# Storing dK and dV of heads 1 to 30 in one 2 MB DMA each, and requesting the third V after the first dV

## The chip, the cores and the metric

The kernel runs on one core of a Trainium2 chip. The core has a matrix engine (TensorE, PE in the profile; its weight loads are PEld), a vector engine (VectorE, DVE), a scalar engine (ScalarE, ACT), GpSimd (POOL) and a sync engine (SP). Sixteen DMA engines move data between the chip's main memory (HBM) and the on-chip memory. Here every DMA of the program is issued by SP. The metric is the device time of one execution in microseconds (us), the median over several runs.

## The reference

It is the forward and backward pass of attention for one query row per head (a decode step): 32 heads, 8192 keys and values per head, head size 128, everything in bf16.

```python
def _fwd_reference(q, k, v):                  # q (1,32,1,128), k and v (1,32,8192,128)
    scale = q.shape[-1] ** -0.5
    scores = jnp.einsum('bhqd,bhkd->bhqk', q, k) * scale
    attn = _softmax(scores, axis=-1)
    return jnp.einsum('bhqk,bhkd->bhqd', attn, v)

_out, _vjp = jax.vjp(_f, q, k, v)
_grads = _vjp(grad_out)                       # dq, dk, dv
```

For one head, with the scores' softmax p (8192 numbers), the outputs are o = p V, dP = V dO, ds = p (dP - dO.o) scale, dq = ds K, dK = ds q (an outer product, 8192 x 128) and dV = p dO (an outer product too). K and V are read once, 2 MB each per head; dK and dV are written once, 2 MB each per head. That makes 268 MB of traffic in all, half read, half written.

## The kernel before

**Tiling.** The 8192 rows of a head lie on 128 partitions, 64 rows to a partition, so a partition's share of K, V, dK or dV is one contiguous run of 16 KB. `Kt` has three buffers, `Vt` two, and the two generated tiles `G_dk` and `G_dv` two each. A head is cut into four quarters for the on-chip work: `outer(h, which, r)` makes quarter r of dK or dV with one VectorE instruction (L207), and `k_blocks(h, u)` transposes a quarter of K on VectorE (L142). V is transposed on TensorE (`v_transposes`, L180) and evacuated by ScalarE (L182).

**Stores.** Inside `outer`, `parts` says in how many pieces the tile is stored: 4 for the last head, otherwise `NST = 2`. So quarters 0 and 1 make the first 1 MB store and quarters 2 and 3 the second (issued at L215). Loads are whole 2 MB DMAs (L75 for K, L81 for V), other than those of head 0, which go in four pieces.

**The loop.** One iteration h works on the scores, the softmax and dV of head h, and on dK and dq of head h-1. The instructions stand in the order in which the program emits them on each engine (`tc.manual_schedule()`). VectorE's order in iteration h: the four transposes of K(h); ds of head h-1; dK quarters 0 to 3 of head h-1, with the small softmax steps of head h between them; then dV quarters 0 to 3 of head h. TensorE's: scores of head h; dq of head h-1 in two halves; softmax sums; the V transposes of head h and the product with V; dP.

**SP's order.** SP issues the DMAs in program order and, at each, waits for what that DMA needs: the data (for a store), a free buffer (for a load), and a free completion semaphore. The trace shows eight such semaphores in rotation, so a DMA can be issued when the one eight places before it has landed. In a middle iteration h the order is: first half of dK(h-1), K(h+2), second half of dK(h-1), first half of dV(h), V(h+2), second half of dV(h). `load_k(h+2)` takes the buffer of K(h-1), last read by `dq_of(h-1, 1)`; `load_v(h+2)` takes that of V(h), last read by TensorE's transposes and product of head h. In iteration 0 there is no dK; K(2) is requested late in it, and V(2) between the second and third quarter of dV(0).

**The ends.** Before the loop SP requests q, grad_out, K(0), V(0), K(1), V(1). After the last load, V(31) in iteration 29, only stores are left. Head 31 stores its dV and dK in four pieces each, and the two small outputs go through `result` (L247).

Of the kernel before, what the change touches and what calls it, by code (L numbers as in the profile page):

```python
# [16 lines left out]
R = 4  # L17
K_BUFS = 3
V_BUFS = 2
NST = 2  # L20
QD = 32


# [1 line left out]
def kernel(  # L25
# [13 lines left out]
    _, H, S, D = k.shape  # L39
# [23 lines left out]
    def rows_of(x, h, c, parts):  # L63
        L = NT // parts
        return x[0, h].rearrange("(p n) d -> p n d", p=P)[:, c * L:(c + 1) * L, :]

    def slots(X, c, parts):
        L = NT // parts
        return X[:, c * L:(c + 1) * L, :]

    def load_k(h):
        Kt[h] = kpool.tile([P, NT, D], BF16, tag="K", name="Kt")
        parts = NCH if h == 0 else 1
        for c in range(parts):
            nc.sync.dma_start(slots(Kt[h], c, parts), rows_of(k, h, c, parts))  # L75

    def load_v(h):
        Vt[h] = vpool.tile([P, NT, D], BF16, tag="V", name="Vt")
        parts = NCH if h == 0 else 1
        for c in range(parts):  # L80
            nc.sync.dma_start(slots(Vt[h], c, parts), rows_of(v, h, c, parts))  # L81
# [55 lines left out]
    def k_blocks(h, u):  # L137


        if u == 0:  # L140
            XK[h] = ktpool.tile([P, CH, NB, NCH, QD], F32, tag="XK", name="XK_sb")
        nc.vector.transpose(XK[h][:, :, :, u, :],  # L142
                            slots(Kt[h], u, NCH).rearrange("p g d -> p (g d)").bitcast(F32).rearrange(
                                "p (g w j) -> p g w j", g=CH, w=NB))

    def k_scores(h):
        x = st[h]
        x["s"] = psS.tile([P, 512], F32, tag="s", name="s_ps")
        out = x["s"][:, 0:NT].rearrange("p (a g) -> p g a", a=NQ)
        cols = XK.pop(h).rearrange("p g w u i -> p (g w u i)").bitcast(BF16).rearrange(  # L150
            "p (g w ui e) -> p g w e ui", g=CH, w=NB, e=2)
        for g in range(CH):
            for c in range(2 * NB):
                nc.tensor.matmul(out[:, g, :], lhsT=cols[:, g, c // 2, c % 2], rhs=q_blk[:, h, c, :],  # L154
                                 start=(c == 0), stop=(c == 2 * NB - 1), skip_group_check=True)

    def s_mask(h):
        x = st[h]
        x["sm"] = small.tile([P, NQ, NCH, CH], F32, tag="sm", name="sm")
        nc.vector.tensor_tensor(  # L160
            x["sm"][:], x["s"][:, 0:NT].rearrange("p (a g) -> p a g", a=NQ).unsqueeze(2)
            .to_broadcast([P, NQ, NCH, CH]),
            in_quad[:].unsqueeze(1).unsqueeze(3).to_broadcast([P, NQ, NCH, CH]), op=ALU.mult)

    def s_swap(h):

        x = st[h]
        x["sn"] = x["s"][:, 128:128 + NT]
        for a in range(NQ):
            nc.tensor.matmul(x["s"][a * QD:(a + 1) * QD, 128:128 + NT], lhsT=lane[:],  # L170
                             rhs=x["sm"][:, a].rearrange("p u g -> p (u g)"),
                             start=True, stop=True, skip_group_check=True)
# [22 lines left out]
    def contract(Xt, rep, out_col, first=0, last=NT):  # L195
        for n in range(first, last):
            nc.tensor.matmul(out_col, lhsT=Xt[:, n, :], rhs=rep[:, n, 0:1],  # L197
                             start=(n == 0), stop=(n == NT - 1), skip_group_check=True)

    def outer(h, which, r):  # L200
        x = st[h]
        if r == 0:
            x[which] = gpool.tile([P, NT, D], BF16, tag=which, name="G_" + which)
        G, dst = x[which], out_2 if which == "dk" else out_3
        rep, row = x["ds"] if which == "dk" else x["p"], x["qd"][:, 0 if which == "dk" else 1, :]
        Q = NT // 4
        nc.vector.tensor_tensor(  # L207
            slots(G, r, 4).rearrange("p n (a b) -> p n a b", b=R),
            slots(rep, r, 4).unsqueeze(2).to_broadcast([P, Q, D // R, R]),
            row.rearrange("p (a b) -> p a b", b=R).unsqueeze(1).to_broadcast([P, Q, D // R, R]),  # L210
            op=ALU.mult)
        parts = 4 if h == H - 1 else NST
        if r % (4 // parts) == 4 // parts - 1:
            c = r // (4 // parts)
            nc.sync.dma_start(rows_of(dst, h, c, parts), slots(G, c, parts))  # L215
# [9 lines left out]
    def ds_of(h):  # L225
        x = st[h]
        pdt = small.tile([P, 1], F32, tag="pdt")
        nc.vector.tensor_copy(pdt[:], x["m"][:, 1:2])  # L228
        x["ds"] = small.tile([P, NT, R], BF16, tag="dsrep", name="ds_rep")
        nc.vector.scalar_tensor_tensor(  # L230
            out=x["ds"][:], in0=x["dp"][:, 0:NT].unsqueeze(2).to_broadcast([P, NT, R]), scalar=pdt[:],
            in1=x["p_s"][:].unsqueeze(2).to_broadcast([P, NT, R]), op0=ALU.subtract, op1=ALU.mult)

    def dq_of(h, half):
        out = st[h]["dp"][:, 128:129]
        contract(Kt[h], st[h]["ds"], out, half * NT // 2, (half + 1) * NT // 2)
        if half == 1:
            nc.scalar.copy(dq_all[:, h:h + 1], out)  # L238
# [10 lines left out]
    for h in range(H + 1):  # L249
        p_ = h - 1  # L250
        if h < H:
            x = st[h] = {}
            for u in range(NCH):
                k_blocks(h, u)
            k_scores(h)
        if h > 0:
            ds_of(p_)
            outer(p_, "dk", 0)
            dq_of(p_, 0)
        if h < H:  # L260
            s_mask(h)
            s_swap(h)
        if h > 0:
            dq_of(p_, 1)
            outer(p_, "dk", 1)
        if 0 < h and h + 2 < H:
            load_k(h + 2)
        if h < H:
            mx = small.tile([P, 1], F32, tag="mx")
            nc.vector.reduce_max(mx[:], x["sn"], axis=AX.X)  # L270
            diag = small.tile([P, P], F32, tag="diag")
            nc.vector.tensor_scalar(diag[:], ident_f[:], mx[:], scale, op0=ALU.mult, op1=ALU.mult)
            x["m"] = psM.tile([P, 512], F32, tag="m", name="m_ps")
            nc.tensor.matmul(x["m"][:, 128:256], lhsT=ones_f[:], rhs=diag[:], start=True, stop=True,  # L274
                             skip_group_check=True)
            rows_bc(h)
        if h > 0:
            outer(p_, "dk", 2)
        if h == 0:
            load_k(2)  # L280
        if h < H:
            nbias = small.tile([P, 1], F32, tag="nbias")
            nc.vector.tensor_reduce(nbias[:], x["m"][:, 128:256], axis=AX.X, op=ALU.max, negate=True)  # L283
            e = small.tile([P, NT], F32, tag="e")
            rs = small.tile([P, 1], F32, tag="rs")
            nc.scalar.activation(e[:], x["sn"], ACT.Exp, bias=nbias[:], scale=scale, accum_out=rs[:])  # L286
            nc.tensor.matmul(x["m"][:, 0:1], lhsT=ones_f[:], rhs=rs[:], start=True, stop=True,  # L287
                             skip_group_check=True)
        if h > 0:
            outer(p_, "dk", 3)  # L290
        if h == H:
            break
        rinv = small.tile([P, 1], F32, tag="rinv")
        nc.vector.reciprocal(rinv[:], x["m"][:, 0:1])  # L294
        x["p"] = small.tile([P, NT, R], BF16, tag="prep", name="p_rep")
        nc.scalar.activation(x["p"][:], e[:].unsqueeze(2).to_broadcast([P, NT, R]), ACT.Copy, scale=rinv[:])  # L296
        x["p_s"] = small.tile([P, NT], F32, tag="p_s", name="p_s")
        nc.vector.tensor_scalar(x["p_s"][:], e[:], rinv[:], scale, op0=ALU.mult, op1=ALU.mult)
        v_transposes(h, 0)
        v_transposes(h, 1)  # L300
        contract(Vt[h], x["p"], x["m"][:, 2:3])
        nc.scalar.copy(o_all[:, h:h + 1], x["m"][:, 2:3])
        v_scores(h, 0)
        v_transposes(h, 2)
        nc.tensor.matmul(x["m"][:, 1:2], lhsT=do_f[:, h:h + 1].to_broadcast([P, P]), rhs=o_all[:, h:h + 1],
                         start=True, stop=True, skip_group_check=True)
        v_scores(h, 1)
        v_transposes(h, 3)
        v_scores(h, 2)
        v_scores(h, 3)  # L310
        outer(h, "dv", 0)
        outer(h, "dv", 1)
        if h + 2 < H:
            load_v(h + 2)
        outer(h, "dv", 2)
        outer(h, "dv", 3)
        if h == H - 1:
            result(o_all, out_0)

# [32 lines left out]
```

## Time and profile before

| | |
|---|---|
| median of 6 runs | 650.8 us (650.63 to 651.25) |
| the profiled execution's own time | 650.65 us |
| its span in the profile | 648.9 us |
| mean granted TensorE clock | 0.619 |
| busy share: TensorE / VectorE / ScalarE | 76% / 79% / 28% |
| DMA queue of SP: bytes, share of 16 engines' span | 268.48 MB, 98.3% |
| mean DMA rate over the span | 416 GB/s |
| loads of 2 MB | 31 of K and 31 of V, 27.2 us from issue to landing |
| stores of 1 MB | 62 of dK and 62 of dV, 25.0 and 25.2 us from issue to landing |

Times in the profile are counted from the start of the span. A busy share is an average over the whole span and says nothing of which engine waits for which; the waits and the chain of work do. A DMA is split over the 16 DMA engines, each of which posts one of sixteen increments of the DMA's semaphore; the DMA has landed when the last of them has. The records of these increments are called the semaphore events below. SPq rows are DMA issues: their time is the instant of the request, not that of the transfer.

### The profile page before, as it was taken

What the parts mean: (1) busy time and instruction counts of PE and PEld (TensorE: products, weight loads), DVE (VectorE), ACT (ScalarE), POOL (GpSimd) and SP (SyncE); (2) the same over time, 40 slices, a digit from 0 to 9 for tenths busy, and PEclk for the clock granted to TensorE, in tenths of its full rate; (3) what the DMA queues carried; (4) which work ended last, traced back from release to release, by engine and by line L of the source; (5) the groups of instructions that cost most, each with busy time, mean ns of one, the idle gap of its engine ahead of it and who ended that gap; (6) DMA issues with size and microseconds to landing.
All of it is one profiled execution on the core that took longest, in us unless ns stands there. A gap on an engine that the chain in (4) does not pass through costs nothing.

```text
span 648.9 us, 21097 instructions
## 1 busy us (share of the span) xinstructions
PE 496.2 (76%) x9705; PEld 463.9 (71%) x9705; DVE 513.6 (79%) x660; ACT 183.1 (28%) x325; POOL 0.7 (0%) x6
## 2 busy tenths in 40 slices
PE   2888888787878768797778787777877878767781
PEld 1888788676868668787668777766867877656781
DVE  5799899798777978778877788777797877887753
ACT  0333232232232222332222322223322233222330
POOL 0000000000000000000000000000000000000000
PEclk9986666577666565656565755676655566656755
DMA  8999999999999999999999999999999999999985
GB/s 336 408 388 429 422 425 425 425 425 427 424 430 425 425 427 425 428 426 429 424 425 427 425 426 427 426 428 427 424 425 427 426 432 422 425 428 425 424 363 226
DMA packets 29368, 269.82 MB, mean 416 GB/s; under 512 B 3424, under 2 KB 3424, under 8 KB 5472
## 3 DMA queue, kind: packets, MB, share of 16 engines
q1 hardware_dynamic: 29280, 268.48, 98.3%
q8 instruction: 76, 1.25, 0.7%
q14 instruction: 12, 0.10, 0.0%
HBM read 134.23 MB, written 134.23 MB: 414 GB/s over the span
## 4 chain that ended last, share of the span: by engine, by line
DMA 68%; PE 16%; DVE 10%; ACT 2%; issue 1%; SPq 0%; DVEq 0%; ACTq 0%
DMA Kt<-in_k_dram 39%; DMA out_dram<-G_dv 29%; DVE XK_sb L142 8%; PE T_ps L180 6%; PE s_ps L154 2%; PE dp_ps L197 2%; PE m_ps L197 2%; PE dp_ps L192 1%; ACT XT_sb L182 1%; PE m_ps L274 1%; DVE G_dv L207 1%; DVE G_dk L207 1%; PE m_ps L287 1%; PE s_ps L170 1%; ACT qd L223 0%
## 5 line engine op out<-in xcount | busy, mean ns | idle before, releaser
L180 PE MATMUL T_ps<-ident_f,Vt 128*128 128x128 f32 x1024 | 211.9, 385 | 0.0
L142 DVE STREAM_TRANSPOSE XK_sb<-Kt 128x1024 f32<-128x1024 f32 x128 | 148.1, 1213 | 65.0 <-DMA Kt<-in_k_dram 64.9
L180 PEld LDWEIGHTS T_ps<-ident_f,Vt 128*128 128x128 f32 x1024 | 188.3, 210 | 0.0
L182 ACT COPY XT_sb<-T_ps 128x1024 f32<-128x1024 f32 x128 | 129.6, 1013 | 136.8 <-PE T_ps L180 136.8
L207 DVE TENSOR_TENSOR G_dv<-p_rep,qd 128x2048 bf16<-128x2048 bf16 x128 | 148.2, 1219 | 14.3 <-DMA out_dram<-G_dv 10.2
L207 DVE TENSOR_TENSOR G_dk<-ds_rep,qd 128x2048 bf16<-128x2048 bf16 x128 | 155.7, 1218 | 1.1
L154 PE MATMUL s_ps<-q_blk,XK_sb 128*128 128x4 bf16 x2048 | 59.6, 168 | 61.1 <-DVE pdt L228 58.4
L154 PEld LDWEIGHTS <-XK_sb 128*128 128x128 bf16 x2048 | 57.0, 104 | 63.4 <-DVE pdt L228 60.6
L192 PEld LDWEIGHTS <-XT_sb 128*128 128x128 bf16 x2048 | 70.7, 103 | 28.5 <-ACT XT_sb L182 27.2
L192 PE MATMUL dp_ps<-do_blk,XT_sb 128*128 128x2 bf16 x2048 | 72.2, 165 | 24.5 <-ACT XT_sb L182 24.5
L197 PE MATMUL dp_ps<-ds_rep,Kt 128*128 128x1 bf16 x2048 | 64.3, 165 | 2.6 <-issue 2.1
L197 PEld LDWEIGHTS <-Kt 128*128 128x128 bf16 x2048 | 59.7, 104 | 8.1 <-issue 8.0
L238 ACT COPY dq_all<-dp_ps 128x1 f32<-128x1 f32 x32 | 5.1, 159 | 207.6 <-PE dp_ps L197 207.6
L197 PEld LDWEIGHTS <-Vt 128*128 128x128 bf16 x2048 | 60.1, 101 | 1.5
L197 PE MATMUL m_ps<-p_rep,Vt 128*128 128x1 bf16 x2048 | 58.6, 165 | 0.0
L287 PEld LDWEIGHTS m_ps<-rs,ones_f 128*128 128x128 f32 x64 | 16.0, 310 | 48.6 <-ACT e L286 48.6
L287 PE MATMUL m_ps<-rs,ones_f 128*128 128x1 f32 x64 | 18.7, 362 | 39.2 <-ACT e L286 39.2
L274 PE MATMUL m_ps<-diag,ones_f 128*128 128x128 f32 x64 | 25.6, 500 | 1.9 <-issue 1.2
L283 DVE TENSOR_REDUCE nbias<-m_ps 128x1 f32<-128x128 f32 x32 | 9.3, 291 | 20.2 <-ACT qd L223 20.2
L296 ACT ACTIVATE p_rep<-e,rinv 128x256 bf16<-128x256 f32 x32 | 16.3, 508 | 30.3 <-DVE rinv L294 30.3
L223 ACT CAST qd<-m_ps 128x256 bf16<-128x256 f32 x32 | 11.9, 372 | 44.9 <-PE m_ps L219 44.9
L230 DVE SCALAR_TENSOR_TENSOR ds_rep<-dp_ps,pdt,p_s 128x256 bf16<-128x256 f32 x32 | 15.5, 484 | 9.0 <-PE dp_ps L192 6.3
(44 smaller groups left out, 153.8 us busy)
## 6 DMA issues: line engine op xcount, KB each, us to landing
Kt<-in_k_dram SPq DMA_DIRECT2D x31, 2048.0 KB, 27.2
Vt<-in_v_dram SPq DMA_DIRECT2D x31, 2048.0 KB, 27.2
out_dram<-G_dv SPq DMA_DIRECT2D x62, 1024.0 KB, 25.2
out_dram<-G_dk SPq DMA_DIRECT2D x62, 1024.0 KB, 25.0
Kt<-in_k_dram SPq DMA_DIRECT2D x4, 512.0 KB, 5.1
Vt<-in_v_dram SPq DMA_DIRECT2D x4, 512.0 KB, 8.2
out_dram<-G_dv SPq DMA_DIRECT2D x4, 512.0 KB, 15.9
out_dram<-G_dk SPq DMA_DIRECT2D x4, 512.0 KB, 9.2
```

The lines of the kernel that those rows point to most:

```text
L142: nc.vector.transpose(XK[h][:, :, :, u, :], slots(Kt[h], u, NCH).rearrange("p g d -> p (g d)").bitcast(F32).rearrange("p (g w j) -> p g w ...
L154: nc.tensor.matmul(out[:, g, :], lhsT=cols[:, g, c // 2, c % 2], rhs=q_blk[:, h, c, :], start=(c == 0), stop=(c == 2 * NB - 1), skip_group ...
L180: nc.tensor.transpose(T_ps[:, i, :], words[:, m * P:(m + 1) * P], ident_f[:])
L182: nc.scalar.copy(X[:], T_ps[:])
L192: nc.tensor.matmul(st[h]["dp"][:, n:n + 2], lhsT=X[:, i, e2, :], rhs=do_blk[:, h, e2, :], start=(e2 == 0), stop=(e2 == 1), skip_group_chec ...
L197: nc.tensor.matmul(out_col, lhsT=Xt[:, n, :], rhs=rep[:, n, 0:1], start=(n == 0), stop=(n == NT - 1), skip_group_check=True)
L207: nc.vector.tensor_tensor(slots(G, r, 4).rearrange("p n (a b) -> p n a b", b=R), slots(rep, r, 4).unsqueeze(2).to_broadcast([P, Q, D // R, ...
L223: nc.scalar.copy(x["qd"][:].rearrange("p a d -> p (a d)"), x["m"][:, 256:512])
L230: nc.vector.scalar_tensor_tensor(out=x["ds"][:], in0=x["dp"][:, 0:NT].unsqueeze(2).to_broadcast([P, NT, R]), scalar=pdt[:], in1=x["p_s"][: ...
L274: nc.tensor.matmul(x["m"][:, 128:256], lhsT=ones_f[:], rhs=diag[:], start=True, stop=True, skip_group_check=True)
L287: nc.tensor.matmul(x["m"][:, 0:1], lhsT=ones_f[:], rhs=rs[:], start=True, stop=True, skip_group_check=True)
L296: nc.scalar.activation(x["p"][:], e[:].unsqueeze(2).to_broadcast([P, NT, R]), ACT.Copy, scale=rinv[:])
```

## The change

The constant `NST` goes. `parts` becomes 4 for head 31, 2 for head 0 and 1 for all others, so `outer` issues a single 2 MB store after quarter 3 for heads 1 to 30. In iteration h (1 to 29) `load_v(h + 2)` stands after quarter 2 of dV(h) rather than after quarter 1; in iteration 0 it stands after quarter 3, behind both halves of dV(0).

```diff
-NST = 2
...
-        parts = 4 if h == H - 1 else NST
+        parts = 4 if h == H - 1 else 2 if h == 0 else 1
         if r % (4 // parts) == 4 // parts - 1:
             c = r // (4 // parts)
             nc.sync.dma_start(rows_of(dst, h, c, parts), slots(G, c, parts))
...
         outer(h, "dv", 0)
         outer(h, "dv", 1)
-        if h + 2 < H:
+        outer(h, "dv", 2)
+        if 0 < h and h + 2 < H:
             load_v(h + 2)
-        outer(h, "dv", 2)
         outer(h, "dv", 3)
+        if h == 0:
+            load_v(2)
```

SP's order in a middle iteration h becomes K(h+2), dK(h-1), V(h+2), dV(h): four DMAs of 2 MB each in place of six. Sixty of the 206 DMAs disappear. The bytes moved, the arithmetic and the buffers stay as they are.

## The prediction

> **What bounds the kernel now.** I read the page's strip of DMA and its queue table first, then SP's issues in order of time, then the waits, then the stretches at the end.
>
> ```profile
> DMA  8999999999999999999999999999999999999985
> GB/s 336 408 388 429 422 425 425 425 425 427 424 430 425 425 427 425 428 426 429 424 425 427 425 426 427 426 428 427 424 425 427 426 432 422 425 428 425 424 363 226
> ...
> q1 hardware_dynamic: 29280, 268.48, 98.3%
> q8 instruction: 76, 1.25, 0.7%
> ```
>
> From the fourth slice to the thirty-eighth the DMA rate stands at 422 to 432 GB/s without a dip, while TensorE and VectorE are at 76% and 79%. The transfers are the bound. In SP's order of issue, one head in the middle:
>
> ```profile
> 230.27 0.33 SPq L215 DMA_DIRECT2D out_dram<-G_dv  x1
> 232.88 0.34 SPq L81 DMA_DIRECT2D Vt<-in_v_dram  x1
> 235.33 0.33 SPq L215 DMA_DIRECT2D out_dram<-G_dv  x1
> 240.19 0.33 SPq L215 DMA_DIRECT2D out_dram<-G_dk  x1
> 242.70 0.34 SPq L75 DMA_DIRECT2D Kt<-in_k_dram  x1
> 245.22 0.33 SPq L215 DMA_DIRECT2D out_dram<-G_dk  x1
> 250.09 0.33 SPq L215 DMA_DIRECT2D out_dram<-G_dv  x1
> ```
>
> Each issue falls some 0.05 us after the landing of the DMA eight places before (the one at 230.27 after K, landed at 230.21 by the semaphore events). So the gaps are the times that the earlier DMAs took in the queue: 4.86 and 4.87 us for a load of 2 MB, but 2.61 + 2.45 and 2.51 + 2.52 us for two stores of 1 MB. A head takes 19.82 us. What VectorE waits for, by the page's costliest groups (the last figures are the idle time before them), and below it the last three of the stretches by time (TensorE, weight loads, VectorE, ScalarE, POOL busy, clock, DMA share, GB/s):
>
> ```profile
> L142 DVE STREAM_TRANSPOSE XK_sb<-Kt 128x1024 f32<-128x1024 f32 x128 | 148.1, 1213 | 65.0 <-DMA Kt<-in_k_dram 64.9
> ...
> L207 DVE TENSOR_TENSOR G_dv<-p_rep,qd 128x2048 bf16<-128x2048 bf16 x128 | 148.2, 1219 | 14.3 <-DMA out_dram<-G_dv 10.2
> ```
> ```profile
> 628.00:640.00 12.00, 6.18 (x126) 5.67 (x124) 5.27 (x6) 3.03 (x7) 0.00 (x0) 0.50 0.78 315
> 640.00:644.00 4.00, 0.00 (x0) 0.00 (x0) 0.00 (x0) 0.00 (x0) 0.00 (x0) 0.50 0.67 269
> 644.00:648.80 4.80, 0.00 (x0) 0.00 (x0) 0.00 (x0) 0.00 (x0) 0.00 (x0) 0.50 0.09 38
> ```
>
> VectorE waits for K, about 2.6 us a head: compute follows the transfers. In the last stretch only 0.09 of the 16 DMA engines is at work: they do not finish together. The semaphore events say how far apart. For the last store of dV(30) the first engine is done at 616.60, the last but one at 631.52, the last at 632.41; for the very last DMA it is 641.73, 646.56 and 647.91. The last engine's landings in the tail follow at 1.23 to 1.26 us per 512 KB, so it has work up to the end. **The bound is the chain of transfers on the slowest DMA engine.** Its landing times jump at some fetches of instructions (76 of 16 KB), and it is slower at stores: over 85 DMAs from 300 to 588 us, its median per head is 4.865 and 4.867 for the loads and 2.523, 2.614, 2.480 and 2.522 for the halves (5.07 a pair). The engine that lands first takes 4.855 and 4.862, and 2.446, 2.459, 2.447 and 2.460 (4.906 a pair).
>
> **The change, part by part.** The sum is made against the profiled execution, 650.65 us (span 648.9), which is 0.15 below the median.
>
> *Sixty pairs of 1 MB stores become sixty stores of 2 MB.* The trace has no 2 MB store. Bounds from the nearest rows, for an ordinary engine: if it takes what a 2 MB load takes, 4.858, the pair's 4.906 falls by 0.048: 60 x 0.048 = 2.9 us. Extrapolated from stores alone (512 KB in 1.245 in the tail on the last engine, 1 MB in 2.453, so 1.208 per further 512 KB) it takes 4.87: 60 x 0.037 = 2.2 us. By the packets' own times (309 ns for 8 KB, 611 for 16 KB, 9 for a semaphore write; eight packets and one semaphore write per DMA and engine) 8 x 7 + 9 = 65 ns a pair: 3.9 us. On the slowest engine, 5.07 to 4.866 gives up to 0.204 a pair, 12.2 us. But that engine would soon no longer be the slowest: the next one ends 1.35 us before it (646.56 against 647.91), and that one gains only the ordinary amount. So the ceiling is the ordinary gain plus 1.35. For this the slowest engine must lose 1.35 of its extra 60 x (5.07 - 4.906) = 9.8 us, 14% of it. I take 2.9, the load's row being the nearest in size, plus 1.3: 4.2 us. Ends kept: 2.2 (nothing of the extra goes) and 5.3 (3.9 + 1.35). A loss isn't excluded; it is a rival below.
>
> Here the page "DMA: Bandwidth & Descriptors" of the Trainium skill (Anatomy of one DMA) would give far more: it fits a DMA as about 2.0 us fixed plus its bytes, which for sixty DMAs fewer is 120 us, were they to run one by one. The trace shows them back to back, with 0.05 us per extra DMA. Against the change speaks the same page's ceiling of 435 GB/s (Specifications): the stretch from 120 to 600 us runs at 426, which as an estimate leaves 480 x (1 - 426/435) = 10 us at most.
>
> *The wait of VectorE for dV.* The first quarter of dV(h) needs the buffer of dV(h-2). Before, its second half landed 12.5 us after K(h) (621.82 against 609.35 in the last iteration). In the new queue, K(h) is followed by dK(h-3), V(h), dV(h-2): about 14.7 us. VectorE reaches that quarter 12.2 us after K (621.54 against 609.38), so it now waits some 2.4 us; the four quarters take 4.63, to 19.4, and K(h+1) lands at 19.5. The wait thus replaces that of 2.6 us for K. Behind it stand the transposes of head h+1, then dK. dK's first quarter is reached 5.3 us after K, and its buffer is free at 4.9: no wait. Cost zero, covered by the depth of the queue.
>
> *The moved requests, queue by queue.* Only SP issues DMAs; POOL's queue is passed by none. V(h+2) waits for TensorE's last transposes of head h, which end 19.5 to 21.5 us after K(h) (609.01 against 589.50 and 251.70 against 230.21), and dV(h) stands behind it on SP, ready at 19.4. Then five 2 MB DMAs, 22 to 24 us of work, lie ahead of them, so the queue is not dry. Were that cover gone, each iteration would lose the lateness plus the latency of a request (about 2 us, first K: request 1.65, first landing 4.84 with 1.28 of transfer). The smallest cover is early: V(3) is issued at 46.49 behind dK(0), whose last half ends at 49.6 on the first engine and 52.8 on the last, 1.1 and 4.3 us after the transfer could start. The first half of dV(1) leaves this gap but isn't needed to fill it. SP's sixty issues of 0.33 us are hidden: SP is waiting anyway.
>
> *Iteration 0.* The second half of dV(0) goes ahead of V(2), at about 25.2 (VectorE ends that tile at 25.1) rather than 29.94. Before, V(2) was requested at 29.57, while the last engine was busy until 33.97; on the middle engine V(2) took 5.91 instead of 4.86. Gain between 0 and 1.05; I take 0, since the last engine never lacked work. V(2) lands 2.5 us later, near 43, and TensorE wants it at about 55.
>
> *The tail.* Of the queue, 16 MB now lie behind K(31) and not 15, so K(31) lands about 2.5 us earlier within the same work. The last engine was busy to the end, so this gains nothing. dK(31) is issued 25.1 us after K(31) (634.40), while the queue lasts 39: no new gap. Cost zero.
>
> Sum: 650.65 - 4.2 = 646.45, on the median's scale 646.6.
>
> **The rivals.** *The stores' extra time belongs to writing, not to the number of DMAs.* Then a 2 MB store takes what two halves take; only 60 semaphore writes of 9 ns go, 0.5 us: 650.3, no change. For it: the slowest engine's extra is in stores alone. Against: ordinary engines take 309 ns for 8 KB against 611 for 16.
>
> *16 KB packets are slower in stores.* This is the rival on the other side. K(2) took 5.19 us on the first engine where others take 4.855, V(2) 5.99; the store running between them was undisturbed at 2.53. If big stores had K(2)'s excess throughout, 5.19 instead of 5.07 (slowest) or 4.906: 60 x 0.12 to 0.28 = 7 to 17 us, 658 to 668. It decides once a 2 MB store takes over 5.07. Against it: all loads after 50 us take 4.86.
>
> *The queue runs dry behind V(h+2).* It would show as gaps after each dV. From the cover of 22 us, this needs TensorE later by more than that; only the early 1.1 us could go, below the noise.
>
> **How the numbers follow.** A kernel like this can be told from no change at about 0.2%, 1.3 us. Forecast, 0.74: 646.6, its own range 645.2 to 648.6 (gains of 5.3 to 2.2, and with up to 0.3 of the early 1.05). Writing itself, 0.13: 649.6 to 651. Slower packets, 0.11; dry queue, 0.02: both above. Faster 0.74, same 0.13, slower 0.13. The range, 644.9 to 650.9, leaves out the slower cases and a little at the bottom, which a larger part of the early 1.05 would reach.
>
> **What would show it.** In the profile after: 2 MB loads still at 4.86 us and stores of 2 MB at 4.85 to 4.95 between issues or landings; VectorE's wait for K down from 65 us to under 20, and that of G_dv for its store up from 10 to some 60; the mean rate up from 416 to 419 GB/s; the next slowest DMA engine close behind the last at the end. I am wrong if stores of 2 MB take 5.07 or more, if GB/s dips in the middle slices, or if another engine's fetches put it behind.

## The result and the profile after

The changed kernel takes 649.17 us (median of 18 runs, 648.42 to 650.02) against 650.83 us for the kernel before (38 runs, 650.33 to 652.34). The ratio is 0.9972, with a 95% interval of 0.9966 to 0.9979: faster by 1.4 to 2.2 us, where 4.2 were forecast. The profiled execution of the changed kernel took 648.37 us (span 646.6), that of the kernel before 650.65.

Nearly all that was said of the structure came. The page's strip of the DMA rate and its queue table, for the changed kernel:

```profile
GB/s 332 412 426 428 425 425 423 427 429 423 425 428 429 430 427 427 427 429 428 428 427 428 429 430 425 430 426 431 426 423 431 428 429 427 425 432 424 423 356 218
...
q1 hardware_dynamic: 20640, 268.48, 98.0%
q8 instruction: 76, 1.25, 0.7%
```

The queue moves the same bytes in 20640 packets rather than 29280, and no middle slice dips: the queue never runs dry. The page's costliest groups, where the last figures are the idle time before the instruction and what ended it:

```profile
L206 DVE TENSOR_TENSOR G_dv<-p_rep,qd 128x2048 bf16<-128x2048 bf16 x128 | 148.2, 1219 | 67.7 <-DMA out_dram<-G_dv 65.2
...
L141 DVE STREAM_TRANSPOSE XK_sb<-Kt 128x1024 f32<-128x1024 f32 x128 | 148.1, 1213 | 5.6 <-DMA Kt<-in_k_dram 5.3
```

VectorE's wait for K fell from 64.9 to 5.3 us, and its wait for the store of dV rose from 10.2 to 65.2: one wait took the place of the other, and the DMA rate did not suffer: from 120 to 600 us it is 427 GB/s (426 before). SP's issues of about one head, in time order:

```profile
308.42 0.34 SPq L80 DMA_DIRECT2D Vt<-in_v_dram  x1
308.86 0.41 SPq L214 DMA_DIRECT2D out_dram<-G_dv  x1
315.57 0.34 SPq L74 DMA_DIRECT2D Kt<-in_k_dram  x1
318.49 0.33 SPq L214 DMA_DIRECT2D out_dram<-G_dk  x1
328.01 0.34 SPq L80 DMA_DIRECT2D Vt<-in_v_dram  x1
```

Before, the issues stood 2.4 to 4.9 us apart, because each waited for the landing of the DMA eight places earlier. Now V and dV go out 0.44 us apart. The waits of SP's queue (what it waited for, total us, times, longest) say what releases them:

```profile
SPq L80 <- PE T_ps L179: 249.8, 30, 9.4
SPq L74 <- PE dp_ps L196: 176.3, 29, 8.4
SPq L214 <- DVE rinv L293: 100.3, 31, 11.6
```

SP now waits for TensorE's last read of a buffer and for VectorE's data, no longer for a DMA's completion. So the gaps between issues no longer give the duration of a DMA, and the durations below are taken from the semaphore events alone. The end, by windows (TensorE, weight loads, VectorE, ScalarE, POOL busy, clock, DMA share, GB/s), after one long window in the middle:

```profile
120.00:600.00 480.00, 384.44 (x7418) 360.05 (x7415) 388.43 (x492) 138.17 (x246) 0.00 (x0) 0.57 1.01 427
628.00:640.00 12.00, 2.37 (x67) 2.01 (x66) 5.11 (x5) 0.89 (x4) 0.00 (x0) 0.50 0.76 309
640.00:644.00 4.00, 0.00 (x0) 0.00 (x0) 0.00 (x0) 0.00 (x0) 0.00 (x0) 0.50 0.23 92
644.00:646.60 2.60, 0.00 (x0) 0.00 (x0) 0.00 (x0) 0.00 (x0) 0.00 (x0) 0.50 0.02 10
```

Here the forecast parted from the chip. The end was to fill up, with the next slowest engine close behind the last. Instead the DMA engines work at a share of 0.23 in the last 6.6 to 2.6 us and of 0.02 after that. The kernel before, counted back from its own end in the same way, has 0.29 and 0.03: the end has hardly changed, and one engine is alone in it. (A share of 0.06 is one engine of sixteen.) The semaphore events of the last DMA, and the time that a DMA engine needs from the landing of K(8) to that of K(28), twenty heads in the middle:

| | first engine done | last but one | last | first engine, 20 heads | last engine, 20 heads | difference |
|---|---|---|---|---|---|---|
| before | 641.73 | 646.56 | 647.91 | 390.74 | 399.23 | 8.49 |
| after | 639.44 | 643.15 | 645.60 | 389.16 | 399.11 | 9.95 |

In the profiled pair the ordinary engine gained 1.58 us in twenty heads and the last one 0.12. The gap between the last and the next at the end is 1.35 us before and 2.45 after. That gap differs from execution to execution: with 1 MB stores the runs below have 2.27, 1.68 and 2.82, with 2 MB stores 0.58 and 1.73, so no trend is shown in it. The twenty heads are steadier, and there the sign stays: the last engine gains less than the first. The profiled execution of the changed kernel is the fastest of its nineteen, so its end alone says little.

### The profile page after: what moved, and what is told of

It is laid out like the page before. It is cut to its first block, busy times and chain, and to the rows that moved or that the text cites. A ratio compares the mean times of both kernels' runs of the same rounds, so it can differ in the third digit from the quotient of the medians.

```text
span 646.6 us, 20978 instructions
## 1 busy us (share of the span) xinstructions
PE 500.5 (77%) x9705; PEld 468.2 (72%) x9705; DVE 513.0 (79%) x660; ACT 183.1 (28%) x325; POOL 0.7 (0%) x6
## 3 DMA queue, kind: packets, MB, share of 16 engines
q1 hardware_dynamic: 20640, 268.48, 98.0%
q8 instruction: 76, 1.25, 0.7%
## 4 chain that ended last, share of the span: by engine, by line
DMA 53%; PE 27%; DVE 14%; ACT 2%; issue 1%; SPq 0%; DVEq 0%; ACTq 0%
DMA Kt<-in_k_dram 48%; DVE XK_sb L141 10%; PE T_ps L179 8%; PE s_ps L153 6%; PE dp_ps L196 5%; DMA out_dram<-G_dv 5%; DVE G_dv L206 2%; PE m_ps L196 2%; PE dp_ps L191 2%; PE s_ps L169 1%; PE m_ps L273 1%; ACT XT_sb L181 1%; PE m_ps L286 1%; DVE G_dk L206 1%; ACT qd L222 1%
## 5 line engine op out<-in xcount | busy, mean ns | idle before, releaser
L179 PE MATMUL T_ps<-ident_f,Vt 128*128 128x128 f32 x1024 | 216.2, 391 | 0.0
L206 DVE TENSOR_TENSOR G_dv<-p_rep,qd 128x2048 bf16<-128x2048 bf16 x128 | 148.2, 1219 | 67.7 <-DMA out_dram<-G_dv 65.2
L179 PEld LDWEIGHTS T_ps<-ident_f,Vt 128*128 128x128 f32 x1024 | 191.8, 213 | 0.0
```

The source lines that it names most:

```text
L179: nc.tensor.transpose(T_ps[:, i, :], words[:, m * P:(m + 1) * P], ident_f[:])
L206: nc.vector.tensor_tensor(slots(G, r, 4).rearrange("p n (a b) -> p n a b", b=R), slots(rep, r, 4).unsqueeze(2).to_broadcast([P, Q, D // R, ...
```

## The experiments

Two questions were to be told apart: which part of the change gives the gain, merging or the order in iteration 0; and what the extra time of the slowest DMA engine depends on: the number of stores (the forecast's step), their bytes, or something else in the kernel. In the expectations, letters stand for the theories of that stage. Ratios are against the kernel before, on the same chip.

### Which part of the change

**Merging alone**: the changed kernel with iteration 0 as before.

```diff
         outer(h, "dv", 1)
+        if h == 0:
+            load_v(2)
         outer(h, "dv", 2)
...
-        if h == 0:
-            load_v(2)
```

> The merged 2 MB stores alone; in iteration 0 the order is that of before (V(2) requested between the second and third quarter of dV(0)). Theory A (the slowest DMA engine pays its extra time for the bytes that it stores, so merging leaves its 5.03 to 5.07 us per 2 MB stored nearly as they are; the gain of the change comes from iteration 0): 650.0 to 651, within 0.8 us of before, and the last landing of dK(0)'s second half at 52 to 53 us as before (50.7 in the changed kernel). Theory B (merging gives the gain): 648.5 to 649.5, like the changed kernel.

Measured: 649.1 us, ratio 0.9971 (0.9960 to 0.9981). That is the changed kernel's ratio: merging gives the whole gain.

**Iteration 0 alone**: the kernel before with the new order of iteration 0.

```diff
-        if h + 2 < H:
+        if 0 < h and h + 2 < H:
             load_v(h + 2)
         outer(h, "dv", 2)
         outer(h, "dv", 3)
+        if h == 0:
+            load_v(2)
```

> Halves as before for all heads; only iteration 0 has the changed order (both halves of dV(0), then V(2)). Theory A: 648.6 to 649.6, about as fast as the changed kernel, with V(2) taking about 4.9 us on the last DMA engine instead of 6.5. Theory B: 650.5 to 651, as before.

Measured: 650.73 us, 0.9998 (0.9989 to 1.0007). Nothing, as forecast. In the profiled execution of before, V(2) took 6.00 us on the first engine, and that engine was 0.95 us later at the last store of dV(30) than here (616.60 against 615.65). Two runs with probes, one of the kernel before and one of this one, tell whether the slow V(2) belongs to the old order. The probes, in both:

```diff
+    probe = consts.tile([16, 16, 2, D], BF16)
...
+        if h <= 14:
+            for n in (4, 5):
+                nc.sync.dma_start(probe[0:n, h, n - 4, :], q.rearrange("b h s d -> (b h s) d")[0:n, :])
```

> The kernel before, with tiny loads of 4 and 5 rows after dV of heads 0 to 14, so that the difference shows when the fifth engine's data have landed. It is the comparison for the next run: the fifth engine is expected not to be the last engine before about 100 us.

> The kernel with only iteration 0 changed, and the same tiny loads. At 45 us all engines are 1.0 to 2.4 us earlier than in the kernel before. If the fifth engine's lead is there too and is lost later, its lag to the first engine grows faster than in the run before this by 1 to 2 us within 150 us; if it never had a lead, the two runs agree on it from the start.

Measured: 650.26 and 651.13 us, one run each. V(2) took 4.61 us on the first engine in the old order, 4.5 to 4.7 in the new one. With merging alone, which has the old order too, it took 5.33. So V(2) is slow in two of three executions of the old order and in none of the new one, but the time does not follow it: the order of iteration 0 is not shown to matter. The fifth engine, which will turn out to be the last, landed at 39.44 against 39.88 us, 101.02 against 101.71, 242.35 against 243.27 and 322.67 against 323.75 in the old and the new order: no lead for the new one. In both runs it is not yet the last at 39 and 60 us, and it is from 122 us on.

With these runs the twenty heads have four executions of 1 MB stores and three of 2 MB stores:

| stores | kernels | first engine | last engine | difference |
|---|---|---|---|---|
| 1 MB | before, iteration 0 alone, both with probes | 390.72 to 390.74 | 399.23, 399.40, 399.28, 399.26 | 8.5 to 8.7 |
| 2 MB | after, merging alone, after with the probes below | 389.16, 388.99, 389.07 | 399.11, 397.77, 398.07 | 10.0, 8.8, 9.0 |

The ordinary engine gains 1.66 us in 40 pairs, 0.042 a pair, and does so evenly. The last one gains 0.2 to 1.5 on the mean of the four (399.29), 1.0 in the mean of the three. Its extra has not shrunk; it is larger by 0.1 to 1.5 us.

### The size of the stores, the other way

**Stores in quarters**: four stores of 512 KB for every head but the first.

```diff
-        parts = 4 if h == H - 1 else 2 if h == 0 else 1
+        parts = 2 if h == 0 else 4
```

> The changed kernel, with dK and dV of heads 1 to 30 stored in four 512 KB DMAs each instead of one. By the packets' own times (4 x 8 x 159 ns for 4 KB against 8 x 611 ns) a 2 MB store costs an ordinary engine 0.2 us more. Theory A in its form 'extra per byte on top of the packets': the slowest engine goes from 5.05 to about 5.25 per 2 MB and the kernel is 12 us slower than the changed one, about 661. Theory A in its form 'a rate limit of that engine's stores, whatever the packets': the slowest engine stays near 5.05 to 5.1, other engines come up to it, and the time is 649 to 653. Theory C (an extra per DMA): the extra grows fourfold, over 20 us slower.

Measured: 676.05 us, 1.0395 (1.0378 to 1.0412), far above both. The middle window of this kernel and two of its SP waits:

```profile
120.00:600.00 480.00, 360.53 (x6950) 336.66 (x6946) 365.79 (x458) 130.07 (x230) 0.00 (x0) 0.57 1.01 404
```
```profile
SPq L214 <- DMA Vt<-in_v_dram: 137.0, 29, 6.3
SPq L214 <- DMA Kt<-in_k_dram: 132.8, 29, 7.0
```

The rate is 404 GB/s at a full DMA share. With eight semaphores in rotation, SP waits for the loads among the last eight DMAs, and eight DMAs now hold some 6.4 MB (ten make the 8 MB of a head; before, six did). The quarters took 1.24 to 1.25 us on the first engine and on the last (1.25 to 1.30 just behind a load), and the 2 MB loads 5.3 to 5.5 in the mean instead of 4.86, on both: here it is the loads that are slow, and no run shows why. So the run does not answer the question: the mix changed with the size. It only shows that the 180 DMAs more than in the changed kernel cost 0.15 us each, not 0.04.

### Which engine is the last

**Tiny loads** of 1 to 15 rows after dV in heads 14 to 28 of the changed kernel; the one of n rows has n data increments.

```diff
+    probe = consts.tile([16, 16, D], BF16)
...
+        if 14 <= h <= 28:
+            n = h - 13
+            nc.sync.dma_start(probe[0:n, n, :], q.rearrange("b h s d -> (b h s) d")[0:n, :])
```

> The changed kernel with one tiny load per head more in heads 14 to 28, of 1, 2, ... 15 rows, to see which DMA engine lands last: a DMA of n rows is expected to run on n engines, so it posts n semaphore events, and the one event that is new from n to n+1 shows the lag of the engine added. If the slowest engine is the sixteenth, none of the 15 has its lag of 8 to 15 us; otherwise the lag appears at the n that adds it. The time should stay within 1 us of the changed kernel.

Measured: 648.54 us, one run. A load of n rows shows n late increments and one update at the issue. That agrees with the Trainium skill, "DMA: Bandwidth & Descriptors" (Why a DMA increments its semaphore by 16 and not by 1): a DMA issued from SP uses the largest number of engines, up to 16, that divides its outer dimension, and of the sixteen the lowest-numbered ones. The trace shows how many engines take part, not which; the numbers of the engines here rest on that page. By it each row count adds one engine to those of the last. Engines 1, 2, 3, 8 and 9 are nearly level, the fourth lags some 3 to 5 us behind the first, the fifth 11 and rising to 15, the sixth, seventh and tenth to sixteenth 10 to 14. **Ten engines lag as a group, six do not, and the fifth is the last.**

**Taking work from the fifth engine**: dV(15) stored as partitions 0 to 67 and 68 to 127, which by the same rule run on 4 and on 15 engines.

```diff
+            if (h, which) == (15, "dv"):
+                for lo, hi in ((0, 68), (68, P)):
+                    nc.sync.dma_start(rows_of(dst, h, c, parts)[lo:hi], slots(G, c, parts)[lo:hi])
+            else:
+                nc.sync.dma_start(rows_of(dst, h, c, parts), slots(G, c, parts))
```

> The changed kernel, with dV of head 15 stored in two DMAs, of partitions 0 to 67 and 68 to 127. If a DMA runs on the largest number of engines up to 16 that divides its count of partitions, 68 go to four engines (17 partitions each) and 60 to fifteen (4 each): engines 1 to 4 get 21 packets of 16 KB instead of 8 (7.9 us more), the others 4 or none (2.4 to 4.9 us less). Theory A (the end is set by the fifth engine, which is last, and the four first ones have 11 to 15 us to spare): 649.2 - 2.4 = 646.8. Theory D (the end is set by all engines together, or by the compute): 649 to 650, no gain.

Measured: 653.31 us, 1.0039 (1.0025 to 1.0052): slower. The events confirm 4 and 15 engines. But the four landed that store 10.9 to 19 us after the one before it, where 17 packets of 0.611 us would take 10.4, and two of them lagged 19.9 and 21.5 us afterwards: they became the last.

**The control**: the same split at partition 64, on all 16 engines, `((0, 64), (64, P))`.

> The same split store, but of partitions 0 to 63 and 64 to 127: both run on 16 engines, 4 packets each, and no engine gets more or less. Theory A: as the changed kernel, 649.2 within 0.8. If it is faster by 2 us, the gain of the uneven split is not from unloading the last engine.

Measured: 651.64 us, 1.0014 (1.0005 to 1.0023), 2.5 us above the changed kernel's 649.17 for one store in two pieces. On the last engine in the profiled execution the pieces took 2.57 and 2.66 us and the DMA after them 6.24 instead of about 4.9. **Two such stores**, dV(15) and dK(20) split 68 and 60, `in ((15, "dv"), (20, "dk"))`:

> The uneven split twice, dV of head 15 and dK of head 20. Theory A: engines 1 to 4 get 15.9 us more; the fourth, which was some 11 us ahead of the last, becomes the last by about 5: 649.2 + 5 = 654, slower than with none and than with one. Theory D: no such turn, 647 or less or unchanged.

Measured: 676.4 us, 1.0387 (1.0364 to 1.0410). At K(24) the last engine lags 38.4 us behind the first, against 12.4 in the changed kernel: that is nearly all of the 27 us. A store cut by partitions has a price of its own, whose cause no run here shows, so these three runs could not test the unloading of one engine. They gave no faster version either.

### What the extra depends on

The next kernels keep the transfers and take the computation away: K and V are loaded in the changed kernel's order, whole stores write zeros, and two VectorE copies of one column per head wait for the loads. dQ, dK, dV and the output are not computed.

**Transfers alone, whole stores.**

```diff
+    def store(which, h):
+        dst = out_2 if which == "dk" else out_3
+        dst = dst[0, h].rearrange("(p n) d -> p n d", p=P)
+        L = NT // PIECES
+        for c in range(PIECES):
+            nc.sync.dma_start(dst[:, c * L:(c + 1) * L, :], G[which][:, c * L:(c + 1) * L, :])
...
+        nc.vector.tensor_copy(seen[:, 0, h:h + 1], t["K", h][:, NT - 1, D - 1:D])
+        nc.vector.tensor_copy(seen[:, 1, h:h + 1], t["V", h][:, NT - 1, D - 1:D])
+        if 0 < h and h + 2 < H:
+            load(k, kpool, "K", h + 2)
+        if h > 0:
+            store("dk", h - 1)
+        if h + 2 < H:
+            load(v, vpool, "V", h + 2)
+        store("dv", h)
```

> The transfers of the changed kernel without its arithmetic: K and V of all heads loaded and 2 MB of zeros stored for each dK and dV, in the order K, dK, V, dV, so the outputs are not computed. Few instructions, so hardly any fetches. If the extra of the fifth engine's stores (5.00 to 5.09 us against 4.87) belongs to that engine, one engine lags by some 64 x 0.17 = 11 us at the end and the time is about 640; if it needs the compute or the fetches, all engines end together within 2 us at 628 to 632.

Measured: 632.43 us, 0.9719 (0.9701 to 0.9737). Its queues, its SP issues and two windows (VectorE, POOL busy, clock, DMA share, GB/s):

```profile
q1 hardware_dynamic: 18528, 268.46, 99.8%
q14 instruction: 2, 0.02, 0.0%
```
```profile
303.65 0.34 SPq L70 DMA_DIRECT2D out_dram<-G_dk  x1
308.64 0.33 SPq L63 DMA_DIRECT2D Vt<-in_v_dram  x1
313.37 0.34 SPq L70 DMA_DIRECT2D out_dram<-G_dv  x1
318.25 0.33 SPq L63 DMA_DIRECT2D Kt<-in_k_dram  x1
323.11 0.34 SPq L70 DMA_DIRECT2D out_dram<-G_dk  x1
```
```profile
120.00:560.00 440.00, 7.03 (x45) 0.00 (x0) 1.00 1.01 431
625.00:630.60 5.60, 0.00 (x0) 0.00 (x0) 1.00 0.28 114
```

There is no q8 row: nothing fetches TensorE's instructions. All DMAs stand 4.7 to 5.0 us apart, the rate is 431 GB/s, and the engines end within 3.1 us of each other. So with no computation there is no laggard, and the transfers alone are 17 us shorter than the kernel.

**Transfers alone, halves**: `PIECES = 2`.

> The transfers alone as in the run before this (zeros stored, nothing computed), but every dK and dV in two 1 MB stores. By the first-landing engine's rows (4.906 against 4.858 per 2 MB) it is 64 x 0.048 = 3.1 us slower than with whole stores (632.4), about 635.5; by the packets' times (65 ns a pair) 4.2 us, 636.6. If halves cost nothing when no compute runs, 632 to 633.

Measured: 635.33 us, 0.975 (0.9725 to 0.9774): 2.9 us more for 64 more DMAs, 0.045 a pair. This is the price of the forecast's first term (0.048), measured by itself.

**Transfers and TensorE**: some 300 products per head on constants, the first on K(h), as many instructions as the kernel's.

```diff
+        nc.tensor.matmul(acc[:, 0:4], lhsT=t["K", h][:, 0, :], rhs=ident[:, 0:4], start=True, stop=True,
+                         skip_group_check=True)
+        for i in range(302):
+            nc.tensor.matmul(acc[:, 4:8], lhsT=ident[:], rhs=ident[:, 0:4], start=True, stop=True,
+                             skip_group_check=True)
```

> The transfers alone, whole stores, plus some 300 matrix products per head on constants, as many TensorE instructions as the kernel has; nothing else is computed. If the instruction fetches make the engines lag, ten of the 16 DMA engines lag by 10 to 14 us at the end, six by less than 5, and the time is 643 to 648. If the fifth engine's extra at stores comes with the fetches too, its stores show 5.0 us or more and it is last. If the lag needs the compute, the time stays at 632.

Measured: 655.93 us, 1.0067 (1.0043 to 1.0091): 23.5 us above the transfers alone. The same views, the windows with TensorE and weight loads ahead of VectorE:

```profile
q1 hardware_dynamic: 18528, 268.46, 96.8%
q8 instruction: 75, 1.23, 0.7%
```
```profile
307.64 0.33 SPq L67 DMA_DIRECT2D Kt<-in_k_dram  x1
313.40 0.34 SPq L74 DMA_DIRECT2D out_dram<-G_dk  x1
318.42 0.33 SPq L67 DMA_DIRECT2D Vt<-in_v_dram  x1
323.13 0.34 SPq L74 DMA_DIRECT2D out_dram<-G_dv  x1
328.01 0.33 SPq L67 DMA_DIRECT2D Kt<-in_k_dram  x1
333.78 0.34 SPq L74 DMA_DIRECT2D out_dram<-G_dk  x1
```
```profile
640.00:645.00 5.00, 0.00 (x0) 0.00 (x0) 0.00 (x0) 0.00 (x0) 1.00 0.14 60
645.00:650.00 5.00, 0.00 (x0) 0.00 (x0) 0.00 (x0) 0.00 (x0) 1.00 0.06 26
650.00:654.00 4.00, 0.00 (x0) 0.00 (x0) 0.00 (x0) 0.00 (x0) 1.00 0.03 13
```

The 75 fetches are back, and so is the lone engine: a DMA share of 0.06 is one engine of sixteen. The issue of dK comes 5.76 us after that of K, and the others 4.7 to 5.0; each such gap is a DMA eight places before on the last engine. By the events dK after K takes 5.79 there, against 4.86 on the last engine with transfers alone and 4.87 on the first engine here: 0.92 to 0.93 more. For dV it is 4.91, as with transfers alone. Nine engines end 12.5 to 16 us behind the first and one 26.2.

**Transfers and VectorE**: the transfers with the kernel's four transposes and eight outer-product quarters per head on VectorE, results unused.

```diff
+        for u in range(NCH):
+            nc.vector.transpose(xk[:, :, :, u, :], ...)
+        for r in list(range(4)) * 2:
+            nc.vector.tensor_tensor(z[:, r * CH:(r + 1) * CH, :]..., op=ALU.mult)
```

> The transfers alone, whole stores, plus VectorE's four transposes of K and eight outer-product quarters per head into a scratch tile: VectorE's main work with few instructions. If VectorE's traffic on the on-chip memory causes the fifth engine's extra at stores, one engine takes 5.0 to 5.1 per 2 MB stored and ends some 10 us behind, at about 640; if not, 632 as with the transfers alone.

Measured: 633.88 us, one run; the last engine ends 4.9 us behind the first. So these instructions of VectorE, without TensorE, make no laggard.

**Transfers and TensorE, halves**: `PIECES = 2` in the kernel with products. This is the run that tells number from bytes.

> The transfers and TensorE's instructions on constants, as in the run with some 300 products per head (655.9), but every dK and dV in two 1 MB stores. Theory A (the last DMA engine's time is set by what TensorE's instructions do to it, not by the count of stores): 656 to 657.5, so that splitting costs clearly less than the 2.9 us that it cost the transfers alone. Theory B (the count of DMAs costs on every engine alike): 658.8.

Measured: 659.23 us, 1.0131 (1.0114 to 1.0148), 3.3 us above whole stores. On the last engine the halves of dK took 2.884 and 2.959, on the first 2.49 and 2.45: 0.91 more per 2 MB, against 0.92 with a whole store. **Twice as many stores, the same extra.** What whole stores save is no part of it: from K(8) to K(24) halves cost the first engine 1.2 to 1.35 us more and the last 1.5 to 1.9, for 32 pairs (against the run with whole stores above and the next one).

**Which engine lags there**: whole stores, and loads of four and of five rows after every fourth head.

```diff
+        if h % 4 == 3:
+            for n in (4, 5):
+                nc.sync.dma_start(probe[0:n, h, n - 4, :], q.rearrange("b h s d -> (b h s) d")[0:n, :])
```

> The same with whole stores, and after every fourth dV two tiny loads, of 4 and of 5 rows, which run on the first four and the first five DMA engines. If the engine that lags by some 26 us at the end is the fifth, as in the changed kernel, the load of 5 rows has one event at that lag and the load of 4 rows none; if it is another engine, neither has.

Measured: 659.35 us, one run. The load of five rows lags 3.29, 6.78, 10.81, 14.30, 17.77, 21.62, 24.90 and 25.36 us, the load of four does not: it is the fifth engine again.

**Half the products**: `range(151)`.

> The transfers and some 150 products per head on constants instead of some 300, whole stores. If the fifth engine's lag grows with TensorE's instructions, it is about half of 26 us at the end and the time lies half-way between 632.4 and 655.9, at 642 to 646. If the lag comes from the wait of each head's products for K and not from their number, it stays at 652 to 656.

Measured: 648.15 us, 0.9953 (0.9933 to 0.9972). Its queue of instructions:

```profile
q8 instruction: 38, 0.62, 0.3%
```

Half the fetches, and nine engines lag 5 to 8 us, half as much. But the last one (the fifth, if it is the same as above) lags 18.6, not 13, and dK after K still takes 5.59 on it. So the lag of the nine goes with the number of fetches, and that of the last does not follow the number alone.

Both halves of this can be read further in the traces. The times of the fetches tell whether the nine wait for them or for TensorE's work as such: between 120 and 580 us of the kernel with all products, the fifteen engines other than the last lose together 1.30 us (median) in each of the 55 DMAs during which a fetch starts (by the landings of the lagging engines), and 0.04 in each of the 40 others. With half the products it is 1.38 (27 DMAs) and 0.00 (68), in the changed kernel 1.23 (58) and -0.03 (37). The last engine's extra at dK goes instead with the time for which TensorE is busy beside that store: 5.28 us with all products, 4.22 with half, for an extra over the first engine of 0.92 and 0.72, so 0.17 us per us in both. Its dV, with TensorE idle, has none, and neither has its load of V, with 2.8 us of TensorE's work beside it. That is two points, no proof, and no single price: in the changed kernel dK has 0.24 for 2.8 us and dV 0.14 for 3.9. Why stores, and why that engine, stays open.

## Why the prediction was right or wrong

*What bounds the kernel.* The transfers, and in them the slowest DMA engine at the end: right. In the profiled executions the last engine ends alone, 1.35 us after the next one before and 2.45 after; with merging alone it is 0.58.

*Sixty pairs of 1 MB stores become sixty stores of 2 MB*, first term, 2.9 us on every engine. The price was right: 2 MB stores take 4.85 to 4.89 us on the first engine (medians of three kernels), as a load does, and the transfers alone gave 0.045 a pair for the 0.048 taken. In the kernel it is 0.042 a pair by the first engine over twenty heads, 2.5 us for sixty; by the last store of dV(30) it is 2.1 (616.60 to 614.51 by merging alone, 615.65 to 613.58 with the new iteration 0 in both). The end shows 1.7, because the last engine gained less than the ordinary one: 1.0 us in the mean over the twenty heads, which is 1.5 for sixty pairs. The Trainium skill's fit of about 2.0 us fixed per DMA, quoted in the prediction from "DMA: Bandwidth & Descriptors" (Anatomy of one DMA), stands there for DMAs issued from GpSimd; SP issues all DMAs here, and no term rested on it.

*"For this the slowest engine must lose 1.35 of its extra ... I take ... plus 1.3"*: **this is the step that failed.** The extra was taken to belong to the number of stores, so that halving the number would remove at least 14% of it. It removed none: over twenty heads the extra is 8.5 to 8.7 us with 1 MB stores and 8.8 to 10.0 with 2 MB. The term of 1.3 should have been zero or below. The ceiling of 1.35 was no firm figure either: it is the gap of one execution, and three others with 1 MB stores have 1.7 to 2.8. The medians of the last engine, for DMAs issued from 150 to 560 us:

| last engine, us | K | V | dK | dV |
|---|---|---|---|---|
| before | 4.867 | 4.863 | 2.522 + 2.613 | 2.466 + 2.517 |
| after | 4.876 | 4.868 | 5.088 | 4.998 |
| merging alone | 4.855 | 4.860 | 5.066 | 4.957 |

The pair of dK was 5.135 and is 5.07 to 5.09, that of dV was 4.983 and is 4.96 to 5.00, which is the ordinary gain of about 0.04 or less; a load's 4.866 was the figure for losing all of it. The experiment with halves and products shows the same by itself: 0.91 and 0.92 us per 2 MB, in two pieces and in one. The prediction had shown that the extra sits in stores alone, and inferred that the number of stores makes it. It had in front of it the fetches of instructions at which that engine's landings jump, and did not ask whether the extra would be there without them. Without TensorE's instructions there is none (4.86 for dK and 4.91 for dV on the last engine, with transfers alone).

*The rival "the stores' extra time belongs to writing".* Half right: true of the slowest engine, whose 2 MB store takes what two halves took, and wrong for the other fifteen. Its 650.3 put this of all engines. The true case stood between it and the forecast: the ordinary gain with no relief of the last engine, which the prediction had kept as its lower end ("nothing of the extra goes") at 2.2 us. The chip gave 1.4 to 2.2.

*"16 KB packets are slower in stores"*, on the other side: no. They take 4.85 to 4.89 on the first engine; on the last 5.09 and 5.00, 5.04 in the mean, below the 5.07 from which this case decides.

*The wait of VectorE for dV.* Right in sign, place and price: K's wait 5.3 (below 20), that for dV 65.2 (some 60), and no cost seen in the rate.

*The moved requests and the dry queue.* Right: no slice dips; 427 GB/s from 120 to 600 us against 426. The rate rose to 417, not 419, since the end is longer than forecast.

*Iteration 0.* Right: zero taken, 0.9998 measured. The 1.05 kept as its upper bound came from a slow V(2) that was there in two executions of the old order and absent in a third, without a trace in the times.

*The tail.* Right: no new gap; the last engine works to the end.

## What to carry to other kernels

When a kernel is bound by transfers, take a DMA's time engine by engine, and ask of any engine's extra what it follows (number of DMAs, bytes, direction, another engine's instructions) before promising to remove it: a change that cuts the number bought here no more than what the ordinary engine shows. Merging queued 1 MB stores into 2 MB is worth 0.04 us a pair here, not more. A probe with the transfers alone, then with one engine's instructions added, shows in two runs whether that engine lengthens them. It does not measure the share in the real kernel: products on constants cost 23.5 us here, more than the 16.7 that the whole kernel takes above its transfers.

## What the runs showed of the hardware that was not expected

- TensorE's instructions compete with the data. Products on constants, which move no data, took the transfers from 632.4 to 655.9 us. They come as 75 fetches of 16 KB (0.7% of the DMA time); ten of the sixteen engines fall behind, nine of them by 12.5 to 16 us, and by 5 to 8 with half the fetches. The loss falls in the DMAs during which a fetch starts, some 1.3 us each. That the fetches run on those engines was inferred from this, not seen.
- The fifth engine is slower still, at stores, above all at the one after K: 0.92 us for each dK with all products, 0.72 with half (on the last engine there), none without. Why that engine, and why at stores, is open.
- One 2 MB store cut into partitions 0 to 63 and 64 to 127 cost 2.5 us; one cut at 68 cost 4.1, two cut at 68 cost 27. Cut along the row, as before the change, a pair costs 0.04.
- Beside 512 KB stores the 2 MB loads took 5.3 to 5.5 us in the mean instead of 4.86, on the first engine and on the last.
